# A new order for the opening of an attention and two-layer mixture kernel, with VectorE spreading the row sums

## The chip, the cores and the metric

The kernel runs on one core of a Trainium2 chip. The metric is device time in microseconds of one execution. A core has five engines with a queue each: TensorE (PE; its weight loads are listed as PEld), VectorE (DVE), ScalarE (ACT), GpSimd (POOL) and SyncE (SP, which here only issues DMAs). Every engine takes its instructions strictly in the order in which they stand, and an instruction that waits holds up all that stand behind it on that engine.

## The reference, cut to what matters

Inputs are q, k, v of 2 batches, 8 heads, 768 positions, 64 per head. The result of the attention, as 1536 tokens of 512, goes through a dense layer pair with a Mish-like gate and then through 8 experts, of which each token takes the one with the largest logit.

```
scores = q @ k.T / sqrt(D) - slope[h] * dist      # only keys within 96 back, and the first 8
a = exp(scores - max); a = a / (sum(a) + 1e-9)
x = a @ v                                         # [1536, 512]
h = x @ w_in;  x = (h * tanh(softplus(h))) @ w_out    # 512 -> 2048 -> 512
e = argmax(x @ w_gate);  out = gate * relu(x @ w1[e]) @ w2[e]
```

w_in and w_out arrive as 64-bit floats and are converted on the chip.

## The kernel before, in words

**Attention.** The 1536 tokens are 12 tiles t of 128. Each tile is worked off in two steps s = 2t and 2t + 1 of four heads each: `a_S` (PE, scores into PSUM tile sp), `a_max` (DVE, adds the distance bias from `ndist` and takes the row maximum, four instructions at L302), `a_exp` (ACT, four exponentials with row sums into su, L313), `a_T` (PE, transposes P, L338/L340), `a_Tev` (ACT, two copies to PT, L353) and `a_V` (PE, times v into av). When both steps of a tile are through, `a_recip` takes 1/sum (DVE, L318/L319) and spreads the eight values over 512 columns (POOL, L321, into tile rs, of which there is one buffer), `a_R` transposes that on PE (L327) and copies it back into rs (ACT, L328), and `a_x` multiplies (DVE, L388), rounds to the high part xh (ACT, L389) and leaves the rest xl (DVE, L390). Two tiles make one block, and the first dense layer needs both tiles of a block.

**Weights.** w_in and w_out come in 32 chunks of 512 KB (wst). A chunk is turned from 64-bit floats into a 32-bit word by three DVE instructions (L167, L169, L171; `next_conv(0)`), rounded by ACT (L205; `next_conv(1)`), and the rest is taken by DVE (L207; `next_conv(2)`). Chunks 0 and 1 make the first quarter pair of w_in that the dense layer needs, 2 and 3 the second, 4 to 7 the matching parts of w_out.

**Dense units.** Each unit u is one block times one eighth of the hidden width: 24 matmuls at L421 (hp), a chain of ACT and DVE work for the gate, and two units later 12 matmuls at L440 (acc). There are 48 units.

**Order.** Up to step s = 4 the instructions of PE, ACT, DVE and POOL stand as the code writes them (`manual_schedule`), but the scheduler may slip instructions of the code behind into the row. From s = 5 a loop takes two steps of attention and one unit per turn, ten turns in all, its order set by the scheduler. Then 38 units without attention follow, and the experts. The opening also builds the bias table (`bias_part`, ten small DVE instructions for each of two pieces, and `bias_copies` on POOL), multiplies q by per-head powers of two (`prep_qk`, L264; tile 0 on DVE, the others on POOL), holds PE warm with 24 matmuls on the identity, and ends with small constants (`make_fast`, `build_consts`).

**Other users.** Tag x2 of pool xe (three buffers) holds the rows of later stages; one of its first users is `prefill`, whose zero tile z is written by POOL (L592) and stored 24 times by SP (L598).

Of the kernel before, what the change touches and what calls it, by code (L numbers as in the profile page):

```python
# [8 lines left out]
F32 = mybir.dt.float32  # L9
# [9 lines left out]
B, H, S, D = 2, 8, 768, 64  # L19
# [22 lines left out]
def moe_kernel(ctx, tc, q, k, v, n_global, n_local, w_in, w_out, w_gate, w1, w2, out, dbg=None):  # L42
# [52 lines left out]

    gorder = [None]

    def bias_copies(nd):
        diag = nd[:, 2 * WN + NG:WC]
        nc.gpsimd.tensor_copy(nd[:, WN + NL:WN + NL + 128], diag)  # L100
        nc.gpsimd.tensor_copy(nd[:, NPRE:WN], diag)
        nc.gpsimd.tensor_copy(nd[:, WN:WN + NL], nd[:, 0:NL])
        gorder[0] = nc.gpsimd.tensor_copy(nd[:, WN + NL + 128:2 * WN], nd[:, NL:NPRE]).ins

# [211 lines left out]
    def a_recip(t):  # L316
        su = rcs.pop(t)
        nc.vector.tensor_scalar_add(su, su, 1e-9)  # L318
        nc.vector.reciprocal(su, su)  # L319
        rbs[t] = at.tile([128, 4, 128], F32, tag="rs", name="rs", bufs=1)  # L320
        gorder[0] = nc.gpsimd.tensor_copy(rbs[t].rearrange("p a (b c) -> p (a b) c", c=64),  # L321
                                          su.unsqueeze(2).to_broadcast([128, H, 64])).ins

    def a_R(t):
        rb = ps.tile([128, 4, 128], F32, tag="b", name="rb")
        for p_ in range(4):
            nc.tensor.transpose(rb[:, p_, :], rbs[t][:, p_, :], ident)  # L327
        nc.scalar.copy(rbs[t], rb)  # L328

    pts = {}  # L330

# [48 lines left out]
    def a_x(t):  # L380
        blk, o = divmod(t, 2)
        cs = slice(o * 128, o * 128 + 128)
        if o == 0:
            xT[blk] = (xblk.tile([128, 4, 256], F32R, tag="xh", name="xh"),
                       xblk.tile([128, 4, 256], F32R, tag="xl", name="xl"))
        xh, xl = xT[blk]
        xm = rbs.pop(t)
        nc.vector.tensor_mul(xm, av_ps.pop(t), xm)  # L388
        nc.scalar.copy(xh[:, :, cs], xm)  # L389
        nc.vector.tensor_sub(xl[:, :, cs], xm, xh[:, :, cs].bitcast(F32))  # L390
        if "x" in dbg:
            for nm, xx in (("x", xh), ("xl", xl)):
                nc.sync.dma_start(dbg[nm][:, t * 128:t * 128 + 128].rearrange("(k p) t -> p k t", p=128),
                                  xx[:, :, cs].bitcast(F32))
        if o == 1:
            for c, xx in enumerate((xh, xl)):
                nc.sync.dma_start(xs[blk, c], xx.rearrange("p k t -> p (k t)").bitcast(F32))

    def x_reload(blk):
        xT[blk] = (xblk.tile([128, 4, 256], F32R, tag="xh", name="xh"),  # L400
# [418 lines left out]
    def next_raw():  # L819
        if nraw[0] < 32:  # L820
            load_raw(*chunks[nraw[0]])
            nraw[0] += 1
# [12 lines left out]
    with tc.manual_schedule(engines={mybir.EngineType.PE, mybir.EngineType.Activation, mybir.EngineType.DVE, mybir.EngineType.Pool}), tc.tile_pool(name="tmp0", bufs=1, side="right") as tmp0:  # L835
        build_scales()
        load_qk(0, 1)
        make_identity(nc, ident)
        warm = ps.tile([128, 512], F32, tag="b", name="warm")

        def fill(n_):
            for _ in range(n_):
                nc.tensor.matmul(warm[:, 0:128], lhsT=ident, rhs=ident, start=True, stop=True)

        fill(NWARM)
        ci = tmp0.tile([128, NG], I32, name="ci")
        bias_iota(ndist, ci)
        load_v(0)
        load_qk(1, 1)
        next_raw()  # L850
        load_v(1)
        load_qk(2)
        next_raw()
        next_raw()
        nl = make_int(nl_raw, "nl")
        ng = make_int(ng_raw, "ng")
        cf = tmp0.tile([128, NG], F32, name="cf")
        nc.vector.tensor_copy(cf, ci)
        gk = tmp0.tile([128, NG], F32, name="gk")
        nc.vector.tensor_scalar(out=gk, in0=cf, scalar1=ng, scalar2=None, op0=ALU.is_lt)  # L860
        for _ in bias_part(ndist, gk, tmp0, 2 * WN, NG + 128, 0):
            pass
        prep_qk(0)
        b1 = bias_part(ndist, gk, tmp0, 0, NPRE, NL)
        a_S(0)
        prep_qk(1)
        for q_ in range(4):
            a_max(0, q_)
        a_S(1)
        for s in range(NS):  # L870
            for q_ in range(2):
                a_exp(s, q_)
            if s:
                if s == 1:
                    fill(4)
                a_T(s - 1, 0)
                a_T(s - 1, 1)
            if s and s + 1 < NS:
                a_S(s + 1)
            if s == 2:  # L880
                prep_qk(2)
            if s == 0:
                for _ in range(6):
                    next(b1, None)
            if s == 4:
                a_x(0)
            if s + 1 < NS:
                a_max(s + 1, 0)
                a_max(s + 1, 1)
            if s:  # L890
                a_Tev(s - 1, 0)
                a_Tev(s - 1, 1)
            if s in (2, 3):
                next_conv(1)
            for q_ in range(2, 4):
                a_exp(s, q_)
            if s + 1 < NS:
                a_max(s + 1, 2)
                a_max(s + 1, 3)
            if s == 0:  # L900
                for _ in range(6):
                    next(b1, None)
                bias_copies(ndist)
            if s in (1, 3):
                a_recip(s // 2)
            if s:
                a_V(s - 1)
            if s in (2, 4):
                a_R(s // 2 - 1)
            if s in (2, 3):  # L910
                next_conv(2)
            if s in (1, 2):
                next_raw()
                next_conv(0)
            if s == 2:
                load_v(2)
            if s == 4:
                load_v(3)
        a_x(1)
        make_fast()  # L920
        build_consts(tmp0)

# [7 lines left out]
    while s <= NST:  # L930
        l1 = L1_mms(u)
        l2 = L2_mms(u - 2) if u >= 2 else iter(())
        for half in range(2):
            def pe(k_):
                if half == 0:
                    run_mms(l1, 2 * k_)
                else:
                    run_mms(l2, k_)

            if s < NST:  # L940
                a_S(s)
            if s % 2 == 1 and s + 1 < NST:
                prep_qk((s + 1) // 2)
            if u < 3:
                next_conv(0)
                next_raw()
                next_conv(1)
            if half == 0:
                chain(u - 1, 4)
                if u % 3 and u > 2:  # L950
                    next_conv(1)
            else:
                chain(u - 1, 9)
                chain(u, 0)
            pe(2)
            if s % 2 == 0 and s > NS:
                a_recip(s // 2 - 1)
            if s < NST:
                a_max(s, 0)
                a_exp(s, 0)  # L960
            pe(1)
            a_T(s - 1, 0)
            a_T(s - 1, 1)
            a_Tev(s - 1, 0)
            a_Tev(s - 1, 1)
            if s < NST:
                a_max(s, 1)
                a_exp(s, 1)
            pe(2)
            if s < NST:  # L970
                a_max(s, 2)
                a_exp(s, 2)
                a_max(s, 3)
                a_exp(s, 3)
            if half == 0:
                chain(u - 1, 5, 6)
            else:
                chain(u, 1)
                chain(u - 1, 10)
            if u < 3:  # L980
                next_conv(2)
            elif half == 0 and u % 3:
                next_conv(2)
            pe(2)
            if s % 2 == 0:
                a_R(s // 2 - 1)
            a_V(s - 1)
            pe(2)
            if s % 2 == 0:
                a_x(s // 2 - 1)  # L990
            if half == 0:
                chain(u - 1, 7, 8)
            else:
                chain(u, 2, 3)
                if (u + 1) % 3 and u > 1:
                    next_conv(0)
                    next_raw()
            pe(3)
            if s % 2 == 0 and 3 < s // 2 + 1 < NTILE:
                load_v(s // 2 + 1)  # L1000
            if s % 2 == 1 and s // 2 + 2 < NTILE and (s // 2 + 2) % 2 == 0:
                load_qk(s // 2 + 2)
            s += 1
        run_mms(l1, 99)
        run_mms(l2, 99)
        if u >= 2 and units[u - 2][2] == PASSES[0][-1]:
            acc_evac(u - 2)
        u += 1
# [392 lines left out]
```

## Time and profile before

| what | value |
|---|---|
| median of 3 runs | 610.17 us (609.69 to 610.38) |
| the profiled execution's own time | 612.11 us |
| its span | 610.4 us |
| busy share PE / DVE / ACT / POOL | 95% / 78% / 62% / 15% |
| mean granted TensorE clock | 0.989 |
| first matmul of a dense unit | 33.37 us after the span's start |

Shares are means over very different stretches. In the 40 slices of 15.3 us that the page shows, DVE is at nine tenths in slices 1 to 3 and again near 90 to 120 us, PE at nine tenths from slice 4 on to the end. A row of the timeline gives start, duration, engine, line, operation, output and inputs; in square brackets stands how long the engine was idle before it and what ended that.

### The profile page before, as it was taken

What the parts mean: (1) busy time and instruction counts of PE and PEld (TensorE: products, weight loads), DVE (VectorE), ACT (ScalarE), POOL (GpSimd) and SP (SyncE); (2) the same over time, 40 slices, a digit from 0 to 9 for tenths busy, and PEclk for the clock granted to TensorE, in tenths of its full rate; (3) what the DMA queues carried; (4) which work ended last, traced back from release to release, by engine and by line L of the source; (5) the groups of instructions that cost most, each with busy time, mean ns of one, the idle gap of its engine ahead of it and who ended that gap; (6) DMA issues with size and microseconds to landing.
All of it is one profiled execution on the core that took longest, in us unless ns stands there. A gap on an engine that the chain in (4) does not pass through costs nothing.

```text
span 610.4 us, 11976 instructions
## 1 busy us (share of the span) xinstructions
PE 582.4 (95%) x4302; PEld 521.8 (85%) x4302; DVE 476.6 (78%) x1143; ACT 379.0 (62%) x882; POOL 93.5 (15%) x167
## 2 busy tenths in 40 slices
PE   8788999999999999999999999998999999999994
PEld 7566877777799989989898989778999999999994
DVE  5999899985689999868767777655895678897942
ACT  3769788878667655564646455555664466676731
POOL 3221111210100101000201201121301112103111
PEclk9979999999999999999999999999999999999998
DMA  7965666689867654431232210277676384586300
GB/s 216 316 231 190 215 243 214 208 249 296 267 221 264 214 189 151 168 109 35 105 104 70 88 52 36 78 273 247 210 264 227 116 304 158 197 304 220 116 17 22
DMA packets 54903, 109.93 MB, mean 180 GB/s; under 512 B 5707, under 2 KB 12875, under 8 KB 54834
## 3 DMA queue, kind: packets, MB, share of 16 engines
q1 hardware_dynamic: 49138, 90.18, 44.1%
q0 software_dynamic: 5696, 18.89, 9.0%
q8 instruction: 36, 0.59, 0.4%
q14 instruction: 33, 0.27, 0.1%
HBM read 84.64 MB, written 25.10 MB: 180 GB/s over the span
## 4 chain that ended last, share of the span: by engine, by line
PE 70%; DVE 12%; ACT 7%; DMA 5%; issue 3%; POOL 1%; SPq 0%; DVEq 0%; POOLq 0%; ACTq 0%
PE hp L421 22%; PE acc L440 18%; PE bhp L704 4%; PE bacc L704 4%; DMA bst<-in_moe_w_dram 3%; PE av L375 2%; PE bhp L705 2%; ACT P L313 2%; PE bacc L705 2%; DVE bw L157 2%; DVE P L302 1%; PE bhp L707 1%; PE bacc L707 1%; PE bacc L709 1%; PE bhp L709 1%
## 5 line engine op out<-in xcount | busy, mean ns | idle before, releaser
L421 PE MATMUL hp<-xh,wpair 128*128 128x256 f32 x768 | 153.4, 289 | 4.6 <-ACT xh L389 4.6
L421 PEld LDWEIGHTS hp<-xh,wpair 128*128 128x128 f32 x768 | 123.5, 190 | 11.1 <-ACT xh L389 6.7
L440 PE MATMUL acc<-wpair,gh 128*128 128x512 f32 x384 | 123.8, 400 | 1.4 <-ACT gh L477 1.4
L421 PE MATMUL hp<-xl,wpair 128*128 128x256 f32 x384 | 109.5, 285 | 1.2 <-DVE xl L390 1.2
L440 PEld LDWEIGHTS acc<-wpair,gh 128*128 128x128 f32 x384 | 68.1, 188 | 16.6 <-issue 3.1
L157 DVE TENSOR_TENSOR bw<-bst,bw 128x512 fp32r<-128x512 f32 x112 | 72.9, 684 | 10.4 <-ACT bw L156 9.6
L448 ACT ACTIVATE e<-hp 128x512 f32<-128x512 f32 x48 | 28.8, 599 | 81.0 <-PE hp L421 80.9
L156 ACT CAST bw<-bst 128x512 fp32r<-128x512 f32 x112 | 64.5, 620 | 22.2 <-PE bhp L708 9.6
L421 PEld LDWEIGHTS hp<-xl,wpair 128*128 128x128 f32 x384 | 73.2, 191 | 3.2 <-DVE xl L390 1.8
L440 PE MATMUL acc<-wpair,gl 128*128 128x512 f32 x192 | 75.4, 393 | 0.0
L704 PE MATMUL bhp<-xc,bw 128*128 128x352 f32 (+4 forms) x192 | 59.4, 365 | 0.6 <-DVE t L739 0.5
L704 PE MATMUL bacc<-hc,bw 128*128 128x352 f32 (+4 forms) x192 | 59.3, 364 | 0.1
L313 ACT ACTIVATE P<-P,mx 128x232 f32<-128x232 f32 (+1 forms) x96 | 44.7, 469 | 13.9 <-DVE mx L302 13.9
L705 PE MATMUL bhp<-xc,bw 128*128 128x176 f32 (+4 forms) x192 | 48.4, 252 | 0.0
L705 PE MATMUL bacc<-hc,bw 128*128 128x176 f32 (+4 forms) x192 | 48.3, 252 | 0.0
L458 DVE SCALAR_TENSOR_TENSOR n<-n,r 128x512 f32<-128x512 f32 x48 | 33.0, 687 | 15.5 <-ACT r L456 15.4
L480 DVE SCALAR_TENSOR_TENSOR gl<-n,gh 128x512 fp32r<-128x512 f32 x48 | 34.3, 715 | 11.7 <-ACT gh L477 10.5
L440 PEld LDWEIGHTS acc<-wpair,gl 128*128 128x128 f32 x192 | 36.0, 188 | 7.5
L704 PEld LDWEIGHTS bhp<-xc,bw 128*128 128x128 f32 x192 | 36.1, 188 | 1.7 <-DVE t L739 0.7
L452 ACT ACTIVATE n<-e 128x512 f32<-128x512 f32 x48 | 30.3, 632 | 11.2 <-DVE e L450 11.0
L704 PEld LDWEIGHTS bacc<-hc,bw 128*128 128x128 f32 x192 | 36.1, 188 | 1.0 <-DVE hc L747 0.3
L705 PEld LDWEIGHTS bacc<-hc,bw 128*128 128x128 f32 x192 | 36.7, 191 | 0.0
(190 smaller groups left out, 1248.6 us busy)
## 6 DMA issues: line engine op xcount, KB each, us to landing
bst<-in_moe_w_dram SPq DMA_DIRECT2D x56, 512.0 KB
wst<-in_moe_w_in_dram SPq DMA_DIRECT2D x16, 512.0 KB
wst<-in_moe_w_out_dram SPq DMA_DIRECT2D x16, 512.0 KB
xl<-xs POOLq DMA_DIRECT2D x12, 512.0 KB, 3.7
xh<-xs POOLq DMA_DIRECT2D x12, 512.0 KB, 4.7
xpl<-xps SPq DMA_DIRECT2D x24, 256.0 KB
xg<-z SPq DMA_DIRECT2D x24, 224.9 KB
w0f<-in_moe_w_dram SPq DMA_DIRECT2D x8, 512.0 KB
```

Source lines behind the costliest of these rows:

```text
L156: nc.scalar.copy(hi, src)
L157: nc.vector.tensor_sub(lo, src, hi.bitcast(F32))
L313: nc.scalar.activation(out=Ps[s][:, q_, 0:w], in_=Ps[s][:, q_, 0:w], func=AF.Exp, bias=mxs[s][:, q_:q_ + 1], scale=-1.0, accum_out=rcs[t][ ...
L375: nc.tensor.matmul(av[64 * j:64 * j + 64, 2 * pr + i, :], lhsT=lh, rhs=rh, start=(c == 0), stop=(c == 1))
L421: yield lambda f=f, kk=kk, wi=wi, xx=xx, cs=cs: nc.tensor.matmul(hp[:, f, :], lhsT=w[:, wi, kk, cs], rhs=xx[:, kk, :], start=(kk == 0 and ...
L440: yield lambda f=f, o=o, cs=cs, gi=gi, wi=wi, first=first, last=last: nc.tensor.matmul(accs[b][o], lhsT=gi[:, cs], rhs=w[:, wi, f, :], sta ...
L448: nc.scalar.activation(out=e, in_=hp, func=AF.Exp, scale=-1.0)
L452: nc.scalar.activation(out=n, in_=e, func=AF.Square)
L458: nc.vector.scalar_tensor_tensor(out=n, in0=n, scalar=0.25, in1=r, op0=ALU.add, op1=ALU.mult)
L480: nc.vector.scalar_tensor_tensor(out=gl, in0=n, scalar=-(2.0 ** -80), in1=gh.bitcast(F32), op0=ALU.mult, op1=ALU.subtract)
L704: nc.tensor.matmul(o[:, 0:2 * cap], lhsT=wh, rhs=xc, start=first, stop=False)
L705: nc.tensor.matmul(o[:, 0:cap], lhsT=wl, rhs=xh, start=False, stop=last)
```

## The change

`a_recip` now spreads the sums by a DVE copy into a tile of tag x2; `a_R` leaves its result in PSUM, and the copy back (ACT) is a helper of its own, `a_Rc`, into a second x2 tile. The loop that wrote the opening is replaced by a list: scores of steps 0 and 1, all four maxima and all four exponentials of a step together, then conversions between the later steps, `a_x` of both tiles, and steps of tile 2 behind them. Only chunks 0 and 1 are converted ahead of `a_x(1)`: its last instruction is returned, and the next three conversions are tied behind it (`issue_after`). The multiplication of q for tile 0 moves ahead of the last four of the first ten bias instructions.

```
-        rbs[t] = at.tile([128, 4, 128], F32, tag="rs", name="rs", bufs=1)
-        gorder[0] = nc.gpsimd.tensor_copy(rbs[t].rearrange("p a (b c) -> p (a b) c", c=64),
-                                          su.unsqueeze(2).to_broadcast([128, H, 64])).ins
+        sp_ = xe.tile([128, ROW], F32, tag="x2", name="sp_")[:, 0:DM]
+        nc.vector.tensor_copy(sp_.rearrange("p (a b) -> p a b", b=64), su.unsqueeze(2).to_broadcast([128, H, 64]))
+        rbs[t] = sp_
...
-        nc.scalar.copy(rbs[t], rb)
+        rbs[t] = rb
+
+    def a_Rc(t):
+        rs = xe.tile([128, ROW], F32, tag="x2", name="rs")[:, 0:DM].rearrange("p (a b) -> p a b", a=4)
+        nc.scalar.copy(rs, rbs[t])
+        rbs[t] = rs
...
+        some(b0, 6)
         prep_qk(0)
+        some(b0, 5)
         a_S(0)
+        a_S(1)
         prep_qk(1)
...
+        bias_diag(ndist)
+        heads(a_max, 0)
+        heads(a_exp, 0)
+        heads(a_max, 1)
+        some(b1, 11)
+        bias_copies(ndist)
...
+        heads(a_max, 2)
+        a_recip(0)
+        prep_qk(2)
+        a_S(3)
+        heads(a_exp, 2)
...
+        a_recip(1)
+        a_Rc(0)
+        a_Tev(3, 0)
+        a_Tev(3, 1)
+        a_V(2)
+        a_R(1)
+        a_V(3)
+        load_v(3)
+        a_S(4)
+        next_conv(2)
+        next_conv(1)
+        a_x(0)
+        a_Rc(1)
+        next_conv(2)
+        xlast = a_x(1)
+        heads(a_max, 4)
+        heads(a_exp, 4)
         make_fast()
         build_consts(tmp0)
...
             if u < 3:
-                next_conv(0)
+                with tc.issue_after(xlast):
+                    next_conv(0)
```

The queue of DVE from the reciprocal of tile 1 on, before (cv is a chunk under conversion, the number behind wst tells the chunk: 166, 175, 177, 309, 362 are chunks 0 to 4; av times rs is `a_x`):

```order
L318 TENSOR_SCALAR su_286<-su_286 128x8
L319 RECIPROCAL su_286<-su_286 128x8
L207 TENSOR_TENSOR wpair0_0_311<-cv_364,wpair0_0_311 128x512
L388 TENSOR_TENSOR rs_298<-av_300,rs_298 128x512
L207 TENSOR_TENSOR wpair1_0_489<-cv_490,wpair1_0_489 128x512
L167 TENSOR_SCALAR cv_564<-wst_309 128x512
L390 TENSOR_TENSOR xl_430<-rs_298,xh_429 128x4x128
L169 SCALAR_TENSOR_TENSOR cv_564<-wst_309,cv_564 128x512
L167 TENSOR_SCALAR cv_638<-wst_362 128x512
L171 SCALAR_TENSOR_TENSOR cv_564<-wst_309,cv_564 128x512
L169 SCALAR_TENSOR_TENSOR cv_638<-wst_362,cv_638 128x512
L388 TENSOR_TENSOR rs_405<-av_407,rs_405 128x512
```

The same place in the changed kernel (its line numbers; sp_ is the spread tile, P_453 belongs to step 4):

```order
L320 TENSOR_SCALAR su_301<-su_301 128x8
L321 RECIPROCAL su_301<-su_301 128x8
L323 COPY sp__399<-su_301 128x512
L209 TENSOR_TENSOR wpair0_0_341<-cv_342,wpair0_0_341 128x512
L395 TENSOR_TENSOR rs_401<-av_321,rs_401 128x512
L397 TENSOR_TENSOR xl_441<-rs_401,xh_440 128x4x128
L209 TENSOR_TENSOR wpair0_0_341<-cv_393,wpair0_0_341 128x512
L395 TENSOR_TENSOR rs_445<-av_406,rs_445 128x512
L397 TENSOR_TENSOR xl_441<-rs_445,xh_440 128x4x128
L304 ISA P_453,mx_454<-sp_432,ndist_100 128x232
```

The rest of chunk 2 and the steps on chunks 3 and 4 no longer stand between the two tiles' multiplications; the spread does, and the maxima of step 4 have moved from far ahead to behind.

The queue of ACT from the end of step 1 on, before (128x232 exponentials are those of steps 2 and on, four to a step):

```order
L205 CAST wpair_0_311<-cv 128x512
L313 ACTIVATE P,su<-P,mx 128x232 x2
L328 COPY rs<-rb 128x512
L313 ACTIVATE P,su<-P,mx 128x232 x2
L353 COPY PT<-pt 104x512
L353 COPY PT<-pt 128x512
L205 CAST wpair_0_311<-cv 128x512
L313 ACTIVATE P,su<-P,mx 128x232 x4
L205 CAST wpair_0_489<-cv 128x512
L389 CAST xh<-rs 128x4x128
```

And in the changed kernel:

```order
L315 ACTIVATE P,su<-P,mx 128x232 x4
L360 COPY PT<-pt 8x512
L360 COPY PT<-pt 128x512
L315 ACTIVATE P,su<-P,mx 128x232 x4
L207 CAST wpair_0_341<-cv 128x512
L360 COPY PT<-pt 104x512
L360 COPY PT<-pt 128x512
L334 COPY rs<-rb 128x512
L360 COPY PT<-pt 104x512
L360 COPY PT<-pt 128x512
L207 CAST wpair_0_341<-cv 128x512
```

All eight exponentials of tile 1 now stand ahead of the first cast of a weight chunk.

## Rows read from the trace of the kernel before

**Rows 1.** Stretches: length, busy us of PE, PEld, DVE, ACT, POOL, then PEclk, DMA, GB/s

```profile
14.60:34.10 19.50, 14.83 (x121) 9.59 (x120) 19.30 (x56) 14.93 (x47) 5.33 (x9) 0.89 0.94 305
34.10:60.00 25.90, 22.17 (x183) 17.80 (x181) 23.70 (x78) 20.75 (x59) 4.75 (x8) 0.95 0.59 201
60.00:130.00 70.00, 68.44 (x541) 55.20 (x542) 67.21 (x184) 57.18 (x154) 9.59 (x11) 0.98 0.66 220
130.00:168.00 38.00, 36.17 (x285) 28.54 (x285) 23.54 (x66) 28.35 (x73) 5.72 (x6) 1.00 0.92 284
168.00:500.00 332.00, 327.17 (x2383) 301.57 (x2382) 255.14 (x531) 189.61 (x375) 44.30 (x78) 1.00 0.46 159
```

**Rows 2.** Timeline of PE in the opening

```profile
2.13 7.46 PE L843 MATMUL warm<-ident 128*128 128x128 f32 x48 [2.13 <-POOL ident masks.py:199]
...
27.95 1.37 PE L375 MATMUL av<-PT,vv 104*64 104x128 f32 x16 [2.13 <-ACT PT L353]
...
33.37 0.58 PE L421 MATMUL hp<-xh,wpair 128*128 128x256 f32 x1 [1.39 <-ACT xh L389]
```

**Rows 3.** Timeline of ACT in the opening

```profile
16.41 1.05 ACT L353 COPY PT<-pt 8x512 f32<-8x512 f32 x2
19.09 0.62 ACT L205 CAST wpair<-cv 128x512 fp32r<-128x512 f32 x1 [1.62 <-DVE cv L171]
19.61 0.48 ACT L313 ACTIVATE P<-P,mx 128x232 f32<-128x232 f32 x1
...
25.39 0.47 ACT L313 ACTIVATE P<-P,mx 128x232 f32<-128x232 f32 x1
```

**Rows 4.** Timeline of DVE in the opening

```profile
14.61 0.40 DVE L302 CUSTOM_DVE_ANT_0 P<-sp,ndist 128x232 f32<-128x232 f32 x1 [0.56 <-ACT PT L353]
...
14.94 0.39 DVE L302 CUSTOM_DVE_ANT_0 P<-sp,ndist 128x232 f32<-128x232 f32 x1
...
17.64 1.41 DVE L171 SCALAR_TENSOR_TENSOR cv<-wst,cv 128x512 int32<-128x512 int32 x1
...
26.68 0.68 DVE L207 TENSOR_TENSOR wpair<-cv,wpair 128x512 fp32r<-128x512 f32 x1
27.28 0.42 DVE L167 TENSOR_SCALAR cv<-wst 128x512 int32<-128x512 int32 x1
27.61 0.68 DVE L390 TENSOR_TENSOR xl<-rs,xh 128x512 fp32r<-128x512 f32 x1
...
29.86 1.52 DVE L171 SCALAR_TENSOR_TENSOR cv<-wst,cv 128x512 int32<-128x512 int32 x1
...
31.99 0.68 DVE L388 TENSOR_TENSOR rs<-av,rs 128x512 f32<-128x512 f32 x1
...
33.35 0.69 DVE L390 TENSOR_TENSOR xl<-rs,xh 128x512 fp32r<-128x512 f32 x1
...
39.04 1.10 DVE L207 TENSOR_TENSOR wpair<-cv,wpair 128x512 fp32r<-128x512 f32 x1
```

**Rows 5.** Timeline of POOL in the opening

```profile
17.03 1.48 POOL L264 TENSOR_TENSOR qr<-qr,qsc 128x512 f32<-128x512 f32 x1
28.46 0.92 POOL L321 COPY rs<-su 128x512 f32<-128x512 f32 x1 [9.95 <-DVE xl L390]
...
29.62 1.20 POOL L264 TENSOR_TENSOR qr<-qr,qsc 128x512 f32<-128x512 f32 x1
...
38.66 0.94 POOL L321 COPY rs<-su 128x512 f32<-128x512 f32 x1 [2.65 <-DVE su L319]
```

**Rows 6.** Waits of DVE from 34 to 130 us, the longest

```profile
DVE e L450 <- ACT e L448: 1.9, 3, 0.8
```

**Rows 7.** Stretches: two microseconds of the opening

```profile
32.00:34.00 2.00, 0.63 (x3) 0.63 (x4) 1.95 (x8) 1.32 (x5) 0.00 (x0) 0.50 0.75 217
```

**Rows 8.** Timeline of the DMA queue SP

```profile
126.94 9.39 SPq L598 DMA_DIRECT2D xg<-z  x12
...
175.68 0.38 SPq L181 DMA_DIRECT2D wst<-in_moe_w_in_dram  x1
```

More of the change, by code (lines that the diff above doesn't have):

```diff
@@ L96, in moe_kernel, with bias_diag @@
     gorder = [None]
-    def bias_copies(nd):
+    def bias_diag(nd):
         diag = nd[:, 2 * WN + NG:WC]
@@ L101, in bias_copies @@
         nc.gpsimd.tensor_copy(nd[:, NPRE:WN], diag)
+    def bias_copies(nd):
         nc.gpsimd.tensor_copy(nd[:, WN:WN + NL], nd[:, 0:NL])
@@ L326, in a_R @@
         for p_ in range(4):
-            nc.tensor.transpose(rb[:, p_, :], rbs[t][:, p_, :], ident)
-        nc.scalar.copy(rbs[t], rb)
+            nc.tensor.transpose(rb[:, p_, :], rbs[t][:, p_ * 128:p_ * 128 + 128], ident)
+        rbs[t] = rb
[3 more added lines that the diff above has]
+        rbs[t] = rs
     pts = {}
@@ L389, in a_x @@
         nc.scalar.copy(xh[:, :, cs], xm)
-        nc.vector.tensor_sub(xl[:, :, cs], xm, xh[:, :, cs].bitcast(F32))
+        ins = nc.vector.tensor_sub(xl[:, :, cs], xm, xh[:, :, cs].bitcast(F32)).ins
         if "x" in dbg:
@@ L397, in a_x @@
                 nc.sync.dma_start(xs[blk, c], xx.rearrange("p k t -> p (k t)").bitcast(F32))
+        return ins
     def x_reload(blk):
@@ L860, in moe_kernel, with some, heads @@
         nc.vector.tensor_scalar(out=gk, in0=cf, scalar1=ng, scalar2=None, op0=ALU.is_lt)
-        for _ in bias_part(ndist, gk, tmp0, 2 * WN, NG + 128, 0):
-            pass
+        def some(it, n_):
+            for _ in range(n_):
+                next(it, None)
+        def heads(f, s_, qs=range(4)):
+            for q_ in qs:
+                f(s_, q_)
+        b0 = bias_part(ndist, gk, tmp0, 2 * WN, NG + 128, 0)
+        b1 = bias_part(ndist, gk, tmp0, 0, NPRE, NL)
+        some(b0, 6)
         prep_qk(0)
-        b1 = bias_part(ndist, gk, tmp0, 0, NPRE, NL)
+        some(b0, 5)
@@ L865, in moe_kernel @@
         a_S(0)
+        a_S(1)
         prep_qk(1)
[L867 to L913, printed above, removed]
-                next_conv(0)
[L915 to L918, printed above, removed]
@@ L919, in moe_kernel @@
-        a_x(1)
+        bias_diag(ndist)
[4 more added lines that the diff above has]
+        bias_copies(ndist)
+        fill(4)
+        a_T(0, 0)
+        a_T(0, 1)
+        heads(a_exp, 1)
+        a_S(2)
+        a_Tev(0, 0)
+        a_Tev(0, 1)
+        a_T(1, 0)
+        a_T(1, 1)
+        heads(a_max, 2)
[3 more added lines that the diff above has]
+        heads(a_exp, 2)
+        a_V(0)
+        a_Tev(1, 0)
+        a_Tev(1, 1)
@@ new lines, in moe_kernel @@
+        heads(a_max, 3)
+        next_raw()
+        next_conv(0)
+        a_T(2, 0)
+        a_T(2, 1)
+        heads(a_exp, 3)
+        a_V(1)
+        load_v(2)
+        a_T(3, 0)
+        a_T(3, 1)
+        a_R(0)
+        next_conv(1)
+        a_Tev(2, 0)
+        a_Tev(2, 1)
+        next_raw()
+        next_conv(0)
+        a_recip(1)
[8 more added lines that the diff above has]
+        next_conv(2)
@@ L920, in moe_kernel @@
+        next_conv(1)
+        a_x(0)
[4 more added lines that the diff above has]
+        heads(a_exp, 4)
         make_fast()
@@ L944, in moe_kernel @@
             if u < 3:
-                next_conv(0)
+                with tc.issue_after(xlast):
+                    next_conv(0)
                 next_raw()
@@ L986, in moe_kernel @@
                 a_R(s // 2 - 1)
+                a_Rc(s // 2 - 1)
             a_V(s - 1)
```

## Prediction

> **What bounds the kernel now.** I read the stretches first, then the timelines of PE, ACT, DVE and POOL in the opening, then the waits of DVE, then the DMA queue. From 168 us on PE is busy 327.17 of 332.00 us and nobody else comes near [rows 1]: that part can't move, so whatever the change does must show as an earlier or later start of it. From 60 to 130 us PE (68.44 of 70.00) and DVE (67.21 of 70.00) are both nearly full [rows 1]. From 14.6 to 34.1 DVE is busy 19.30 of 19.50 us while PE has 4.7 us of gaps [rows 1]: there DVE is the bound, and PE waits. The first dense matmul starts at 33.37 us, and PE waited 1.39 us for ACT's xh [rows 2]. From 130 to 168 DVE has slack (23.54 of 38.00) [rows 1]. So the question is not only how early the first dense matmul comes, but how much of DVE's work has been done by then, because DVE stays full until about 130 us.
>
> Why does the first dense matmul come only at 33.37? The maxima of tile 1 begin at 14.61 on DVE [rows 4], but two of its exponentials stand behind a weight cast on ACT, which waits 1.62 us for DVE's conversion: the cast is at 19.09, the exponential at 19.61, and the tile's last exponential ends at 25.39 + 0.47 = 25.86 [rows 3]. Then the spread of tile 1 waits on POOL until 28.46, because rs has one buffer, still read by the xl of tile 0 that starts at 27.61 [rows 4, 5]. Its product stands on DVE behind conversions of chunks 3 and 4, one of which takes 1.52 us, and comes at 31.99 [rows 4].
>
> **The change, part by part.** Durations: a DVE operation overlaps the next, so I count from start to start. Two sources in SBUF, 128x512: 27.28 - 26.68 = 0.60. One source: 27.61 - 27.28 = 0.33. One maximum: 14.94 - 14.61 = 0.33 [rows 4]. ACT: exponential 0.47, pair of PT copies 1.05, cast 0.6 [rows 3].
>
> *Ahead of 14.61.* The same bias instructions and eight maxima stand in another order, with the same sum, and the scores of step 2 still need POOL's copies of the bias. Bringing q's scaling forward four small steps gives nothing: PE is in its warm-up matmuls until 2.13 + 7.46 = 9.59 and can't take scores sooner [rows 2]. Zero.
>
> *From 14.61 to the first dense matmul.* DVE: four maxima 1.3 (15.9), sum, reciprocal and spread at 0.33 each, 1.0 (16.9), four maxima (18.3), chunk 0 as 0.33 + 0.60 + 0.60 = 1.5 (19.8), chunk 1 (21.3), reciprocal and spread of tile 1 (22.3), rest of chunk 0 0.60 (22.9), product (23.5). ACT beside it: four exponentials from 15.0 (16.9), PT (17.9), four exponentials (19.8), cast (20.4), PT, the copy of rs, PT, cast (23.7), xh of tile 0 (24.3). Then xl (24.9), rest of chunk 1 (25.5), product of tile 1 (26.1), xh (26.7) and two handovers: 27.0. The last exponential of tile 1 would end at 19.8, six microseconds sooner. POOL's scaling of q for tiles 2 and 3 now runs without a spread ahead of it, somewhere after 14.6; an L171 beside POOL's L264 took 1.41 and 1.52 against a step of 0.60 [rows 4, 5], so two collisions make 28.6 at most. I take half of one: 27.4, between 27.0 and 28.6. The first dense matmul leads by 33.4 - 27.4 = 6.0 us, and xl of tile 1, which ended at 34.0 [rows 4], ends near 28.1, 5.9 earlier.
>
> *What is owed.* When the kernel before ended that xl, it had also done work that now stands behind: four maxima of step 4 (1.3), two of step 5 (0.7), all of chunk 2 (1.5 + 0.6) and two instructions of chunk 3 (0.9), together 5.0. So DVE is ahead by only 5.9 - 5.0 = 0.9 us. **-0.9.**
>
> *DVE's idle time.* DVE idled 25.90 - 23.70 = 2.2 us from 34 to 60 and 2.8 us from 60 to 130 [rows 1], in waits for ACT and, through it, PE, as the 1.9 us before L450 [rows 6]. With PE and ACT six microseconds ahead and DVE one, the operands should lie ready. Bounds nothing and all; I take 1.8 of the first, where the lead is fresh, and 1.2 of the second. **-3.0.**
>
> *The spread on DVE.* 134 us hold ten more tiles, so seven fall before 130, where DVE is full; the others fall into slack. No DVE operation in this trace reads one value 64 times over. The nearest row is L167, one source, SBUF to SBUF, every second word of its source: 0.33; the other end is 0.60. I take 0.33, times seven. **+2.3**, up to +4.2.
>
> *The spread off POOL.* L207 took 1.10 while POOL spread at 38.66, 0.42 more than 0.68 [rows 4, 5]. Seven of that are 2.9, none is 0; I take a third, because much of what DVE does in a step, the maxima above all, reads its scores from PSUM and not two operands from SBUF. **-1.0.**
>
> The Trainium skill has a rule on each. "VectorE: DVE Perf Modes", section "Mode 2×_2P", says that a one-source operation between SBUF operands with an even outermost dimension gives two results a cycle even in fp32; L167 agrees, no run here shows it for a repeated source; by it the sum below stands, without it it would be about -0.7. "SBUF — State Buffer", section "Who interferes with whom", speaks against the change: a copy in that mode holds the port pair that DVE and GpSimd share for its whole length, so spreads and POOL's scaling would go on blocking each other; by it the relief is gone and the sum is -1.6.
>
> *Other edits.* The early maxima and exponentials of steps 4 and 5 come later than the matmul, so unit 0's matmuls, between which step 4's transposes stand, wait for them; hidden, since PE waits for DVE there anyway. The gaps of 2.13 and 1.39 us [rows 2] go with a PEclk of 0.50 from 32 to 34 us [rows 7]; the layout leaves no such gap before 27.4, but I count nothing for it while DVE is the bound. The tile z is now written on POOL behind the first reload of x, as the attention ends, instead of at the start, so its 24 stores, of which twelve took the queue 9.39 us from 126.94 on, come when weight loads like that at 175.68 stand behind them [rows 8]. Those loads feed chunks that are needed only in the second half of the dense units; nothing, at worst 1 us. Releasing POOL and rs brings nothing else: x2 has three buffers.
>
> Sum: -0.9 - 3.0 + 2.3 - 1.0 = **-2.6 us**. The profiled execution goes from 612.11 to 609.5; the median shown lies 1.94 lower, so the forecast is 610.17 - 2.6 = **607.6 us**. Ends: -0.9 - 5.0 + 2.3 - 2.9 = -6.5 and -0.9 + 4.2 = +3.3.
>
> **Rivals.**
> *PE keeps its lead.* If from 34 to 130 us PE rather than DVE sets the pace, all 6.0 us stay: 604.2. For it: PE is as full as DVE from 60 on [rows 1], and conversions owed are of chunks needed later. Against it: DVE at 23.70 of 25.90 before that.
> *All handed back.* DVE waits as often as before, only elsewhere, since each xl still waits for ACT's xh: -0.9 + 2.3 - 1.0 = +0.4, 610.6. For it: a loop in which three engines wait for each other in turn keeps its waits when one gets a lead. This is also the case in which the list does what it says and it is worth nothing.
> *VectorE pays.* The spread takes the slow end, 0.60, on the engine that is full, no idle time is recovered and no relief comes: -0.9 + 4.2 = +3.3, 613.5. It decides if the copy's step is over 0.5 us and DVE's idle time from 60 to 130 stays near 2.8. Against it: the L167 row, and seven spreads of POOL that no longer disturb.
>
> **How the numbers follow.** Forecast 0.50, PE's lead 0.13, handed back 0.21, VectorE pays 0.16. The measurement can tell 0.2%, 1.2 us, from no change. Faster: most of the forecast case (0.43) and PE's lead, 0.56. Within: what is left of the forecast and the handed-back case, 0.27. Slower: 0.17. The range 604.0 to 612.0 leaves out the slow rival and a little beyond PE's lead. The forecast's own range is 605.5 to 609.7.
>
> **What would show it.** Right: first dense matmul between 27.0 and 28.6; tile 1's last exponential near 20 us; the copy of the spread at 0.4 us and steps of 0.33; DVE's idle time from there to 125 us about 2 instead of 5; last xl of the attention 2 to 3 us earlier; from there on the same 332 us of PE. Wrong: a first matmul after 30, a spread of 0.68, gaps on PE of over 2 us behind the first dense unit with a PEclk of 0.50, or a stall of PE behind the stores of z after 168 us.

## The result, and the profile after

| | before | after |
|---|---|---|
| median | 610.27 us (609.69 to 610.70) | 602.62 us (602.29 to 603.13) |
| ratio after/before, 95% interval | | 0.9871 [0.9853, 0.9889] |
| profiled execution / span | 612.11 / 610.4 | 602.45 / 600.7 |
| first dense matmul starts | 33.37 | 27.25 |
| xl of tile 5 / of tile 11 ends | 87.52 / 167.3 | 82.63 / 159.6 |

The gain is 7.65 us where 2.6 were forecast, and the time lies below the range. The spans differ by 9.7 us: the dense units keep a distance of 7.65 us (one starts at 372.99 before and at 365.34 after), and the last 2 us lie behind the dense units, in the routing and experts. The profiled execution before was itself 1.84 us over its median. In the experiments below medians are of all executions, and ratios leave out two single executions, of 1118 us (debt_early) and 3147 us (z_front), that are unlike all others.

The opening went as forecast. (Where xl of a tile has a time below, that is the end of the instruction that writes it.) Timeline of PE after (start, duration, engine, line, operation, output and inputs; idle time before it and what ended it), to [rows 2]:

```profile
27.25 0.38 PE L429 MATMUL hp<-xh,wpair 128*128 128x256 f32 x1 [0.97 <-ACT xh L396]
```

ACT's last exponential of tile 1, to [rows 3]:

```profile
18.86 0.47 ACT L315 ACTIVATE P<-P,mx 128x232 f32<-128x232 f32 x1
```

DVE, to [rows 4]: the spread, its next instruction, tile 1's xl, and right behind it the maxima of step 4:

```profile
22.34 0.43 DVE L323 COPY sp__399<-su 128x512 f32<-128x512 f32 x1
22.68 0.68 DVE L209 TENSOR_TENSOR wpair<-cv,wpair 128x512 fp32r<-128x512 f32 x1
...
27.23 0.69 DVE L397 TENSOR_TENSOR xl<-rs,xh 128x512 fp32r<-128x512 f32 x1 [0.68 <-ACT xh L396]
27.84 0.39 DVE L304 CUSTOM_DVE_ANT_0 P<-sp,ndist 128x232 f32<-128x232 f32 x1
```

What the forecast did not see is behind that. Stretches of after (length, busy us of PE, PEld, DVE, ACT, POOL, then PEclk, DMA, GB/s), to [rows 1]:

```profile
27.20:60.00 32.80, 28.62 (x238) 23.30 (x240) 32.45 (x104) 27.15 (x77) 5.20 (x7) 0.95 0.74 242
60.00:120.00 60.00, 57.20 (x462) 45.25 (x458) 57.82 (x161) 51.02 (x138) 5.59 (x5) 1.00 0.57 196
120.00:160.00 40.00, 39.24 (x312) 31.39 (x311) 33.18 (x93) 32.04 (x82) 2.10 (x6) 1.00 0.60 199
160.00:500.00 340.00, 336.57 (x2445) 310.59 (x2444) 263.95 (x549) 195.96 (x389) 46.00 (x81) 1.00 0.51 175
```

DVE idles only 32.80 - 32.45 = 0.35 us from the first dense matmul to 60 us. The slack at the end of the attention, 14.5 us from 130 to 168 before [rows 1], is down to 6.8 from 120 to 160. From 160 us on PE is as full as it was. So work went from the front of the attention to its end. Two more stretches, from 14.6 us to the end of tile 5's xl and from there to that of tile 11, first of before, then of after:

```profile
14.60:87.52 72.92, 63.76 (x512) 49.58 (x510) 68.63 (x197) 57.39 (x160) 13.82 (x22) 0.93 0.70 233
87.52:167.30 79.78, 77.16 (x610) 60.94 (x611) 64.44 (x183) 63.82 (x169) 11.56 (x12) 1.00 0.79 252
```

```profile
14.60:82.63 68.03, 59.93 (x512) 47.13 (x512) 65.18 (x194) 55.74 (x154) 14.18 (x19) 0.97 0.71 231
82.63:159.60 76.97, 75.88 (x607) 60.37 (x605) 68.86 (x195) 64.59 (x171) 2.10 (x6) 1.00 0.62 209
```

DVE's idle time is the length less its busy time, 72.92 - 68.63 = 4.29 us before and 68.03 - 65.18 = 2.85 after. To tile 5 DVE works 68.63 - 65.18 = 3.45 us less and idles 1.44 less: together the 4.9 us by which that xl is early. Behind it DVE works 4.4 us more (68.86 against 64.44), and the stretch is still 2.8 us shorter. The reason for the smaller work is in the order of DVE's instructions. Chunks whose last step (L207 before, L209 after) stands ahead of each tile's xl:

```
tile            0   1   2   3   4   5   6   7   8   9  10  11
before          3   3   6   8  11  13  15  18  20  20  20  20
after           1   2   4   6   8  10  12  15  17  19  20  20
behind by       2   1   2   2   3   3   3   3   3   1   0   0
```

The debt, one finished chunk at tile 1, is not paid in the stretch where DVE is full. It grows to three and is paid between the xl of tile 8 and that of tile 10, where DVE has time (33.18 of 40.00 us busy from 120 to 160). Three chunks are 3 x 2.13 = 6.4 us (0.33 + 3 x 0.60 each, by [rows 4]); six spreads at 0.33 are 2.0 the other way. That would make 4.4 us less work where 3.45 were measured; the difference is not followed up here.

### The profile page after: what moved, and what is told of

It is laid out like the page before. It is cut to its first block, busy times and chain, and to the rows that moved or that the text cites. A ratio compares the mean times of both kernels' runs of the same rounds, so it can differ in the third digit from the quotient of the medians.

```text
span 600.7 us, 11943 instructions
## 1 busy us (share of the span) xinstructions
PE 577.4 (96%) x4302; PEld 519.4 (86%) x4302; DVE 478.1 (80%) x1155; ACT 378.8 (63%) x882; POOL 83.7 (14%) x155
## 4 chain that ended last, share of the span: by engine, by line
PE 73%; DVE 13%; ACT 8%; DMA 3%; issue 1%; POOL 1%; SPq 0%; DVEq 0%; POOLq 0%
PE hp L429 21%; PE acc L448 18%; PE bhp L712 5%; PE bacc L712 5%; ACT P L315 2%; PE bhp L713 2%; PE bacc L713 2%; DVE P L304 2%; PE bhp L731 2%; PE bhp L715 1%; PE bacc L715 1%; PE av L382 1%; PE bacc L717 1%; ACT PT L360 1%; PE bhp L717 1%
## 5 line engine op out<-in xcount | busy, mean ns | idle before, releaser
L712 PEld LDWEIGHTS bhp<-xc,bw 128*128 128x128 f32 x192 | 36.1, 188 | 1.7 <-DVE t L747 0.8
L713 PEld LDWEIGHTS bhp<-xc,bw 128*128 128x128 f32 x192 | 36.7, 191 | 0.0
```

The costliest lines, as they stand in the source:

```text
L712: nc.tensor.matmul(o[:, 0:2 * cap], lhsT=wh, rhs=xc, start=first, stop=False)
L713: nc.tensor.matmul(o[:, 0:cap], lhsT=wl, rhs=xh, start=False, stop=last)
```

## Experiments

The theory after the result: **the order of the conversions** gives as much as the early opening, because DVE sets the pace up to tile 5 and what stands on it ahead of a tile counts; later TensorE sets it (this last part is argued, not tested). The rivals: **PE's lead**, that an earlier first dense matmul is kept whatever DVE does, **the spread**, that taking it off POOL is the larger part, and **TensorE's clock**, that fewer stretches at half the clock are. The last can't be put aside by size: by PEclk above (the share of full speed that was granted, 1.00 for 2.4 GHz and 0.50 for 1.2), the stretch to tile 5 lost 0.07 x 72.92 = 5.1 us of full-speed time before and 0.03 x 68.03 = 2.0 after. Ratios are to the kernel before on the same chip; the other columns are from each run's trace (us).

| kernel | median | ratio, 95% interval | first dense matmul | xl of tile 5 | xl of tile 11 |
|---|---|---|---|---|---|
| changed, again | 603.51 | 0.9892 [0.9867, 0.9917] | 27.7 | 82.4 | 160.9 |
| tie_alone | 606.67 | 0.9933 [0.9910, 0.9956] | 33.0 | 83.0 | 162.3 |
| spread_alone | 609.63 | 0.9979 [0.9956, 1.0002] | 35.3 | 90.2 | 167.4 |
| tie_spread | 607.61 | 0.9939 [0.9919, 0.9959] | 33.1 | 86.7 | 164.6 |
| list_alone | 605.84 | 0.9902 [0.9876, 0.9928] | 27.4 | 83.9 | 162.3 |
| debt_early | 612.32 | 1.0015 [1.0000, 1.0031] | 27.8 | 90.6 | 168.2 |
| debt_behind | 605.44 | 0.9899 [0.9872, 0.9925] | 27.4 | 82.6 | 159.7 |
| late_conv | 621.63 | 1.0185 [1.0155, 1.0215] | 27.1 | 81.9 | 160.1 |
| warm_gap | 610.20 | 0.9983 [0.9965, 1.0001] | 33.1 | 86.6 | 166.4 |
| fill_gap | 605.18 | 0.9903 [0.9877, 0.9929] | 27.7 | 82.3 | 160.8 |
| steady | 618.45 | 1.0125 [1.0103, 1.0147] | 27.0 | 81.0 | 160.9 |
| steady_fill | 620.40 | 1.0156 [1.0130, 1.0181] | 27.5 | 80.8 | 160.8 |
| fix5 | 612.38 | 1.0021 [1.0001, 1.0040] | 27.7 | 80.0 | 159.3 |
| fix5_z | 605.88 | 0.9904 [0.9885, 0.9924] | 27.4 | 80.0 | 159.2 |
| after_z | 604.55 | 0.9881 [0.9863, 0.9899] | 27.2 | 81.9 | 159.3 |
| z_front | 605.56 | 0.9909 [0.9889, 0.9928] | | | |

**The changed kernel again**, as the base of the variants.

> The changed kernel unaltered, beside the variants on the same chip, as their base: 602.6 if the chip makes no difference; the kernel before was 610.3 in the first comparison and 611.1 in the second.

603.51. The ratio is 0.9892 where the first comparison had 0.9871; the two intervals overlap.

**tie_alone: the tie without the rest** (before's list, POOL's spread).

```
-        a_x(1)
+        xlast = a_x(1)
...
             if u < 3:
-                next_conv(0)
+                with tc.issue_after(xlast):
+                    next_conv(0)
```

> The kernel before with nothing changed but that the three conversions that follow the opening are tied behind xl of tile 1: chunk 2's and 3's steps no longer stand between the two tiles' products on VectorE, and by tiles 2 to 4 it has 2, 4, 6 chunks behind it instead of 3, 6, 8. Two of those steps took 1.5 us each before 32 us, so the first dense matmul should come at 30 to 31 us instead of 33.4. If a lead of the opening stays, whoever is owed what: 607.5 to 609. If VectorE's debt is paid back in the full stretch, as the forecast had it: 610 to 611.

The mechanism expected is refuted, and the result is the clearest of the study. The first dense matmul came at 33.0, no earlier, because tile 1's product now waits for rs (waits of DVE from 14.6 to 34 us: total, times, longest):

```profile
DVE rs L388 <- ACT rs L328: 3.6, 1, 3.6
```

And yet xl of tile 5 comes 4.6 us earlier and the run gains 4 us. The row of chunks ahead of the xl is 2, 2, 4, 6, 8, 11, 14, 16, 18, 20: like after's, not like before's. The stretch to tile 5:

```profile
14.60:83.00 68.40, 62.08 (x521) 47.61 (x520) 62.50 (x191) 56.79 (x160) 13.29 (x24) 0.98 0.69 226
```

DVE idles 5.9 us of it, 1.6 more than before, nearly all ahead of 34 us, and then hardly at all (25.77 of 26.00 us busy to 60, 22.97 of 23.00 to 83). But it works 6.1 us less. So more than half of the gain needs no earlier opening. PEclk is 0.98 here against 0.93 before; what of the 4.6 us came by the clock is not told apart by this run.

**debt_early: chunks 2 and 3 converted ahead of the maxima of step 4** in the changed kernel.

```
         xlast = a_x(1)
+        for _ in range(2):
+            next_conv(0)
+            next_raw()
+            next_conv(1)
+            next_conv(2)
         heads(a_max, 4)
...
-            if u < 3:
+            if 0 < u < 3:
```

> The changed kernel, but chunks 2 and 3 are converted right behind xl of tile 1 and ahead of the maxima of step 4, as in the opening before; the order up to that xl is the same. By the tiles 3 to 9, VectorE then has 1 to 2 chunks more behind it than in the changed kernel (5, 7, 10, 11, 14, 16, 19 instead of 4, 6, 8, 10, 12, 15, 17), which is the debt that the forecast said would be paid in the full stretch. If postponing that work is what keeps the lead, the time rises by 1 to 2 chunks of 2.1 us less what idle time takes up: 604 to 606.5, and the lead of xl of tiles 3 to 6 over the kernel before falls from 7 to about 3 to 5 us. If VectorE's amount of work doesn't matter there, 602.3 to 603.2.

Worse than any theory had it: the first dense matmul is at 27.8, and the whole gain is gone. The stretches show why, here debt_early, then the changed kernel:

```profile
34.00:38.00 4.00, 1.18 (x5) 0.78 (x6) 3.96 (x20) 3.97 (x11) 1.46 (x2) 0.50 0.94 316
38.00:42.00 4.00, 3.26 (x16) 1.76 (x17) 4.00 (x17) 3.03 (x12) 0.89 (x3) 0.50 0.24 89
42.00:46.00 4.00, 4.00 (x23) 2.99 (x20) 2.21 (x11) 0.79 (x3) 0.00 (x0) 0.50 0.00 0
```

```profile
34.00:38.00 4.00, 3.32 (x34) 2.29 (x32) 4.00 (x17) 3.43 (x10) 0.35 (x2) 1.00 0.43 127
38.00:42.00 4.00, 4.00 (x35) 3.70 (x35) 4.00 (x11) 3.97 (x11) 0.00 (x0) 1.00 0.98 317
```

With the maxima behind two chunks of conversions (the first at 35.69 instead of 27.84) TensorE has nothing to do (5 matmuls in 4 us), the granted clock falls to 0.50, and when work comes it is done at 1.2 GHz for 8 us more, now with DVE waiting for scores (3.7 us from 34 to 54). An early first matmul is not enough; how much of the loss is the place of the conversions and how much the clock behind it, this run does not tell.

**debt_behind: the same loop, issued behind the maxima and exponentials of step 4.**

> The changed kernel with the conversions of chunks 2 and 3 issued right behind the maxima and exponentials of step 4, where the kernel that issued them ahead of those maxima lost the whole gain (612.3). By each xl as many chunks are through as in the changed kernel, but the first steps of both come some 10 instructions earlier on VectorE. If the loss there was the place ahead of the maxima (TensorE starved, and its clock halved from 34 to 47 us), the gain is back: 603 to 605. If it was VectorE's work paid early, whatever its place, 606 to 609.

The gain is back, and xl of tile 5 is where the changed kernel has it although xl of tile 2 came 1.5 us later (43.3 against 41.8): the same 10 chunks stand ahead of tile 5 in both. So the loss of debt_early came from the place of the two chunks, with the starved TensorE that it caused. With tie_alone this supports the theory as far as tile 5: the maxima first, and few chunks ahead of a tile. It also speaks against the clock in the changed kernel: from 14.6 to 160 us PEclk is 1.00 in debt_behind and 0.98 in the changed kernel again (0.02 x 145.4 = 2.9 us), and the ratios are 0.9899 and 0.9892.

**spread_alone: the spread on VectorE in the old list.** Its edits are those of a_recip, a_R and a_Rc in the change.

> The kernel before with only the spread on VectorE, in x2 tiles, with the copy back as a helper of its own; the old list of the opening. The zero tile leaves the front of POOL with it. By the forecast's sizes +2.3 - 1.0, and about -0.45 for the earlier start: 611.1. If the list is the whole gain and the spread nothing, 610.3 less the earlier start: 609.8. If the spread off POOL and rs with more than one buffer were the larger part, 606 or less.

Not told from no change. The first dense matmul comes 1.9 us later and xl of tile 5 2.7 us later than before, but the stretch from there to tile 11 takes 77.2 us instead of 79.8:

```profile
90.20:167.40 77.20, 76.25 (x607) 60.33 (x606) 65.89 (x189) 64.47 (x170) 2.10 (x6) 1.00 0.60 198
```

**list_alone: the changed kernel with the spread on POOL.**

```
-        nc.vector.tensor_copy(sp_.rearrange(...), su.unsqueeze(2).to_broadcast([128, H, 64]))
+        gorder[0] = nc.gpsimd.tensor_copy(sp_.rearrange(...), su.unsqueeze(2)...).ins
```

> The changed kernel with the spread of the row sums issued on POOL again (into the same x2 tiles, so the zero tile stays at the end); everything else as changed. By the forecast's sizes VectorE loses 0.33 us for each of seven tiles (-2.3) and collides with POOL again (+1.0): 601.3. If POOL's spread is on the path (it took 0.92 us against 0.42, and stands between the reciprocal and the transposes), up to 7 x 0.5 = 3.5 us more: 603 to 606. If the end's slack takes either, 602.6.

The expectation of 603 to 606 holds, but by time it isn't told from the changed kernel (0.9902 against 0.9892). Its trace has what POOL's spread costs at one tile: at tile 2 it took 1.15 us, TensorE waited 1.32 us for it, and from 38 to 42 us PEclk was 0.57.

**tie_spread: tie and spread, the old list.**

> The kernel before with the tie of the conversions behind xl of tile 1 and the spread on VectorE, so with everything of the change except the list of the opening (and its early scaling of q). With the tie alone VectorE waited 3.61 us for rs ahead of tile 1's product; the spread on VectorE should take that wait, so the first dense matmul comes near 30 us instead of 33.0. If the list is worth only its earlier first matmul (27.7 against 30), 604 to 606, between the tie alone (606.7) and the changed kernel (603.5 in this comparison). If the order of the conversions is all of the gain, 603.0 to 604.0. If the spread on VectorE costs what the forecast gave it, 607 to 608.

Slower than expected with the earlier opening, since that did not come: tile 1's exponentials still end at 26.7, V of step 3 waits 2.48 us for ACT's PT behind tile 0's xh, and DVE 2.4 us for rs, so the first dense matmul stays at 33.1. Up to tile 5 it has no more chunks ahead than tie_alone (2, 2, 4, 6, 8, 10), and yet that xl comes 3.8 us later. DVE idles as much (5.9 us) and works nearly that much more:

```profile
14.60:86.70 72.10, 62.30 (x518) 48.12 (x519) 66.16 (x193) 56.92 (x158) 16.07 (x21) 0.97 0.68 219
```

Six spreads are part of it, and four one-source conversion steps (L167) that met POOL's scaling of q and took 1.26 us each instead of 0.42, 3.4 us in all, two of them at 53.66 and two at 81.25. So the row of chunks alone does not give the time; what DVE has to work ahead of the tile does.

From this kernel to the changed one only the list changes: 0.9939 to 0.9892, about 2.9 us. That is the list's own share. At tile 5 it is 4.1 us: DVE idles 3.1 us less (2.85 against 5.94) and works 1.0 less. So from before to after xl of tile 5 moves by -4.6 with the tie, +3.8 with the spread and -4.1 with the list; the order of the conversions and the earlier opening are of the same size.

**late_conv: seven chunks out of the attention.** Conversions of the code behind the attention are tied behind its last xl.

> The changed kernel, but the conversions that the code behind the attention issues are tied behind the attention's last xl: 13 chunks instead of 20 stand ahead of it on VectorE, so 7 x 2.1 = 15 us of VectorE's work leave the stretch from 60 to 160 us. If VectorE's row sets the pace there (60 to 120: 57.82 of 60.00 us busy, PE idle 2.80 us, and 0.76 more to 160), PE gets back most of those 3.6 us: 599.5 to 600.5, against 602.6. If what PE waits for is the chain over three engines and not VectorE's amount of work, nothing moves: 602.0 to 603.0. A third way: chunks 14 and 15 come too late for the units behind the attention, 604 or more, with PE waiting for a wpair tile after 160 us.

The stretches, late_conv, then the changed kernel:

```profile
60.00:160.00 100.00, 96.39 (x770) 76.16 (x767) 74.61 (x221) 79.94 (x212) 8.35 (x11) 1.00 0.44 145
200.00:260.00 60.00, 46.95 (x280) 41.39 (x279) 50.83 (x92) 29.49 (x49) 4.24 (x8) 0.89 0.90 276
```

```profile
60.00:160.00 100.00, 96.45 (x772) 76.64 (x769) 91.00 (x253) 83.06 (x219) 7.70 (x11) 1.00 0.58 197
200.00:260.00 60.00, 60.00 (x383) 54.45 (x382) 53.90 (x92) 34.36 (x57) 5.79 (x12) 1.00 0.57 196
```

From 60 to 160 DVE has 16.4 us less to do and the last xl comes at 160.1, not earlier: there DVE's amount is not the bound, although it was 91% busy. The run loses 18 us behind the attention, where units wait for weights: DVE waits 8.5 us for one, and that load, at 219.16 in the queue SP, stands behind 13 stores of the zero tile (see fix5).

**warm_gap: six matmuls on the identity in PE's pause before 27.95**, in the kernel before.

```
             if s:
+                if s == 4: fill(6)
                 a_V(s - 1)
```

> The kernel before with six matmuls on the identity (they write a tile that nobody reads) in TensorE's pause of 2.13 us before 27.95; every other row of every engine stands as before. There the granted clock is 0.50 from 29.9 to 36.4 us. If the spell at the half clock is part of what the changed list saves, the first unit shortens: first dense matmul at 32.5 to 33.4 us, the second unit 1 to 2 us earlier than 46.6, and the time 608.5 to 609.8 against 610.3 to 611. If VectorE holds the first units up whatever TensorE's clock is, the time stays within 0.3 us; if the pause before 33.37 halves the clock anyway, the same.

The clock stayed up to 34 us (0.96 from 30 to 34 instead of 0.50), and fell to 0.61 from 34 to 38, behind the second pause (0.66 before). The second unit starts at 45.8 instead of 46.6, xl of tiles 5 and 11 come 0.9 us earlier; 0.9983 with an upper end of 1.0001, not told from no change. So 0.46 x 4 - 0.05 x 4 = 1.6 us of full-speed time brought those xl 0.9 us earlier. The other stretches at half the clock in the kernel before were not tested.

**fill_gap: eight such matmuls in the changed kernel before its third unit.**

```
+            if u == 2 and half == 0:
+                warm = ps.tile([128, 512], F32, tag="b", name="warm2")
+                fill(8)
```

> The changed kernel with eight matmuls on the identity in TensorE's pause of 2.74 us before the third unit (at 52.63 us), behind the scores that stand there. In the changed kernel the granted clock is 0.50 from about 52.6 to 56.8. If TensorE's row sets the pace from there on, the 4 us at the half clock are worth up to 2 us: 600.5 to 601.8 against 602.6. If VectorE sets it (25.68 of 26.00 us busy from 34 to 60), no change: 602.3 to 602.9.

From 54 to 58 us the clock is 1.00 instead of 0.57, and xl of tile 4 comes 1.0 us earlier; at tile 5 nothing is left of it (82.3 against 82.4). That agrees with DVE as the bound up to there.

**steady: every turn's conversions tied behind the last xl**, as many by each tile as after.

> The changed kernel, but in every turn of the loop the conversions are tied behind the last xl, two chunks to a turn, so that by each xl the same number of chunks is through as in the changed kernel (1, 2, 4, 6, 8, 10, 12, 14, 16, 18, 20) and none of their first three steps stands just ahead of a tile's product; they stand ahead of the next maxima instead. If the place just ahead of the product is what costs (at tile 5 four such steps stand between 76 and 80 us), xl of tile 5 comes at 79 to 80.5 instead of 82.4 and the time is 600.5 to 602.5 against 603.5. If TensorE's row sets the pace whatever stands there, 603 to 604. If conversions ahead of the maxima starve TensorE, as with chunks 2 and 3 there (612.3), 605 or more.

Xl of tile 5 comes 1.4 us earlier, tile 11's not, and 15 us go later: DVE waits 10.3 us for a weight load. With the filling matmuls added (steady_fill), expected to gain 1 us or nothing, it was 620.4, the same within the scatter.

**fix5: fill_gap with one turn's conversion tied behind xl of tile 5.**

> The changed kernel with the eight matmuls on the identity before the third unit, and with the conversion of one turn tied behind xl of tile 5, so that none stands just ahead of that tile's product; later turns are left to the scheduler, so that weights do not come late behind the attention as they did where every turn was tied. If TensorE's pauses up to tile 5 are worth keeping shut, xl of tile 5 comes at 79 to 80.5 us instead of 82.3 and the time is 601 to 602.5 against 603.5. If what is won there goes in the next turns, 603 to 604.5. If weights come late, 606 or more, with TensorE waiting behind 200 us.

Xl of tile 5 at 80.0, 2.2 us earlier than in fill_gap: 8 chunks stand ahead of it instead of 10. DVE works 8.2 us less there (57.54 against 65.78 us) and idles 7.9, so with this little ahead it no longer sets the pace. Tile 11's xl is at 159.3, and then comes the same trap. Waits of DVE from 190 to 210 us, and the queue SP ahead of that load:

```profile
DVE cv L169 <- DMA wst<-in_moe_w_out_dram: 8.5, 1, 8.5
```

```profile
172.64 11.00 SPq L606 DMA_DIRECT2D xg<-z  x10
...
194.78 0.43 SPq L188 DMA_DIRECT2D wst<-in_moe_w_out_dram  x1
```

**fix5_z and after_z: the zero tile's 24 stores four at a time in the turns 3 to 8**, from a tile of their own.

```
+        if u > 2:
+            some(zst, 4)
-        if u == 16:
-            prefill()
```

> The kernel with the eight matmuls before the third unit and one conversion tied behind xl of tile 5 (612.4, its last xl at 159.3 and then weights late behind the zero stores), and beside that the zero tile in a place of its own and its 24 stores taken four at a time between the loads of the turns 3 to 8, instead of all as the attention ends. If it was the stores that held the weight loads up, the wait of 8.5 us is gone and what the earlier last xl is worth stays: 601 to 603. If the conversions alone are too late, still 610 or more.

> The changed kernel with only the zero tile's stores moved like that, into the turns 3 to 8. If the stores as the attention ends cost the changed kernel nothing, 603 to 604 as in the comparisons before; if they do, less, down to 601; if they hold up the loads of q, k, v and weights in the turns, 605 or more.

In fix5_z the wait is gone (ratio 1.0021 to 0.9904): the loss was the stores. In the changed kernel they cost nothing that can be measured (0.9881 against 0.9892). But its lead of 1.9 us over after_z at tile 5 is gone by tile 11 (159.2 against 159.3): no kernel here brought that xl ahead of 159.2. No variant beat the changed kernel clearly.

**z_front: the zero tile written ahead of the identity again.**

> The changed kernel with the zero tile in a place of its own, written on POOL ahead of the identity, as the kernel before wrote it at the start; its stores are placed by the scheduler again. If the 0.45 us by which the changed kernel's first scores come earlier is that memset (0.51 us on POOL), the first scores come at 9.5 to 9.6 us instead of 9.1, and the whole run 0.4 to 0.6 us later: 604.0 against 603.5. If VectorE's bias table holds the first maxima up anyway, 603.5.

Unclear: the interval of 0.9909 overlaps that of 0.9892, and there is no comparable trace to show when its first scores began.

## Why the prediction was wrong

- **Ahead of 14.61, zero.** In this pair the first scores come 0.42 us earlier (9.10 against 9.52). But kernels with the same opening list began them at 8.70 to 10.13, so that is the scatter of a start, not shown to be the change.
- **First dense matmul 27.4, last exponential near 20, xl of tile 1 at 28.1: right.** 27.25, 19.33, 27.92.
- **What is owed, -0.9: this is the step that failed.** It counted what had not been done at tile 1, and then took for granted that it would be paid while DVE was full, and that DVE sets the pace until about 130 us. The order of the instructions, which was there to be counted, has the debt growing to three chunks and paid between tiles 8 and 10. To tile 5 the lead measured 4.9 us, not 0.9, and behind it DVE's amount is not the bound: 16.4 us less of it moved nothing (late_conv). tie_alone shows that the order behind tile 1 alone is worth 4 us; debt_early and debt_behind show that the place of two chunks alone can cost all of the gain. With 5.9 in place of 0.9 the forecast's own sum would be -7.6 us; that this fits proves little, because its other terms did not come one by one as they were priced.
- **DVE's idle time, -3.0: near in size, but not a saving in time throughout.** From the first dense matmul to 60 us DVE idles 0.35 us where it idled 2.2 from 34.1 on: 1.85 less, forecast 1.8. From 60 on it fell only from 2.79 us to 2.18, forecast 1.2 less, and there DVE's amount was not shown to be the bound. From 14.6 to tile 5, where the opening's own pauses count too, it fell by 1.44.
- **The spread on DVE: right in its step, wrong in its weight.** The copy took 0.43 us, the next instruction began 0.34 later. "VectorE: DVE Perf Modes", section "Mode 2×_2P", of the Trainium skill gives one-source operations between SBUF operands two results a cycle; the trace agrees, for a source that repeats a value, with a step like that of L167 (0.33). But behind tile 5 less work on DVE gained nothing (late_conv), so of the seven that the forecast charged, only the four of tiles 2 to 5 are likely to count. Beside POOL the copy can be slow: 1.12 us at 16.64 in tie_spread, where POOL scaled q from 16.44 to 17.48.
- **The spread off POOL, -1.0: open, the sign too.** From tile 5 to 11 the kernels with the spread on POOL took 79.8 (before), 79.3 (tie_alone) and 78.4 (list_alone); on DVE 77.0 (after), 77.1 (debt_behind), 77.2 (spread_alone), 77.9 (tie_spread), 78.5 in the changed kernel again, and 79.2 to 80.0 in fix5, fix5_z and steady, whose tile 5 was early. By total time the two are not told apart in any pair (before and spread_alone, tie_alone and tie_spread, list_alone and the changed kernel). By the rule of the Trainium skill ("SBUF — State Buffer", "Who interferes with whom"), that DVE and POOL shut each other out at the ports that they share, collisions go on with the spread on DVE. The traces agree that they go on: an L209 beside POOL's L266 took 1.57 us at 32.60 in after, and the four L167 steps of tie_spread 1.26.
- **The zero tile, nothing: right for this kernel, for a thin reason.** Weight loads did stand behind the stores, and fix5, which converted a little later, lost some 7 us by it (1.0021 against 0.9904 with the stores moved). In steady and late_conv, too, the load that DVE waits for stands behind stores of z.
- **The rivals.** PE's lead had the time nearly right, 604.2, and part of its mechanism: from tie_spread to the changed kernel a first dense matmul 5.4 us earlier is kept as 4.1 us at tile 5. But the lead is not kept whatever DVE does (debt_early has it, 27.8, without the gain), and tie_alone has more than half of the gain without it. That this rival's number came near is luck: it lets all 6.0 us of the opening stay and leaves out the order behind it. Handed back and VectorE pays did not happen: the time fell, and the copy's step was 0.34.

What stays open: why the stretch from tile 5 to 11 is 2.8 us shorter after than before, how much of the lead at tile 5 came by TensorE's clock, and what holds xl of tile 11 at 159 to 161 in the kernels with the new list and the spread on DVE (all but debt_early). PE is busy 75.88 of 76.97 us there, which fits TensorE's own work, but no run here took work from it.

## What to carry to other kernels

When a change leaves work behind, count it at every later checkpoint of the engine's order, not only at the first: where it is paid decides what it costs. An engine that is 90% busy sets the pace only up to where its order holds others up; take a large piece of its work away to see it. And a run of bulk stores on a queue may cost nothing that can be measured (after_z) until a load that somebody needs soon stands behind it (fix5).

## What the runs showed of the hardware that was not expected

A pause of TensorE can be followed by a stretch at half the clock: after 2.73 us without matmuls before 53.04 PEclk was 0.57 from 54 to 58 (after_again), and in debt_early the 0.50 lasted from 34 to past 46 us, part of it with PE busy all the time. Eight matmuls that nobody reads kept it at 1.00 (fill_gap), but the time that this won was gone at the next place where DVE set the pace. A one-source step on DVE took 1.26 us instead of 0.42 beside POOL's scaling of q (tie_spread). And a copy on DVE that reads one value 64 times over runs at 0.43 us per 128x512, as one that reads an ordinary source does (0.42).
